# Storing the routing's comparisons and one-hots in groups of six token columns instead of eighteen

## The chip, the cores and the metric

The kernel runs on one core of a Trainium2 chip. The metric is the device time of one execution in microseconds (us); lower is better. TensorE (PE) does matmuls out of on-chip memory into PSUM, VectorE (DVE), ScalarE (ACT) and GpSimd (POOL) do elementwise work, SyncE (SP) issues most transfers.

## The reference

Three blocks follow each other: a masked attention (4 batches, 8 heads, 576 positions, 64 wide; local or strided mask of 32), a mixture of experts with greedy routing over its 2304 tokens, and a dense block on the result:

```python
logits = x @ w_gate                      # [2304, 8]
order = np.argsort(-logits.flatten())    # all (token, expert) pairs, best first
for idx in order:                        # greedy: expert e takes tok unless either is taken or full
    tok, e = (int(idx) // E, int(idx) % E)
    if assigned[tok] >= 0 or counts[e] >= cap:   # cap = 288
        continue
    assigned[tok] = e
    counts[e] += 1
for e in range(E):
    out[assigned == e] = np.maximum(x[assigned == e] @ w1[e], 0) @ w2[e]   # 512 -> 1024 -> 512
h = out @ w_in                           # 512 -> 2048
g = np.where(h > 0, h, np.exp(np.minimum(h, 0)) - 1)
return g @ w_out
```

## The kernel before

**Stages.** Attention fills the first 110 us or so. It leaves each token's eight logits on chip: 2304 tokens as 128 partitions by 18 columns. Then the routing runs in eight phases, each of which fills one expert, and the experts run one after the other in the order in which they are filled. Each expert's 288 tokens are gathered by an indirect DMA, go through the expert (matmuls of 288 columns) and then through the dense block (256, 384 or 512 columns). These matmuls are in single precision by a high and a low part, all issued from line 948. Phase 0 runs alone, with nothing else for PE to do; the routing of a later expert runs while an earlier expert is computed, its matmuls strewn into PE's stream.

**One routing phase.** A phase finds the logit at which the first expert is full by six digits, of 6, 6, 5, 5, 5 and 5 bits, that is K = 63 or 31 thresholds. For one digit DVE compares each token's digit with all thresholds at once (L711), which gives a 0/1 tile `cmp` (a part of `ohU`) in bf16. PE then counts per expert: one matmul for each token column c, whose weights are the column's one-hot of experts `oh[:, c, :]` and whose moving operand is the column's K comparisons (L740), 18 matmuls that add into one PSUM tile `pc`. DVE takes the digit from that (L742 to L757). When the threshold is known, the place of each token among the expert's 288 is worked out (L788 to L803), DVE makes the one-hot of places (L808, 96 wide) and PE uses it as weights, column by column, to bring the token numbers to their places (L818). After phase 3 half of the tokens are left, and `compact` moves them to 9 columns by two bursts of nine matmuls (L902) with the one-hot of L886 and L888 as weights. So phases 1 to 3 work on 18 columns, 4 to 7 on 9. Phase 7 has no digits, only the places.

**The layout.** The comparisons lie as [128, threshold, column], the 18 columns side by side for each threshold, also when only 9 are used. So DVE writes them in long runs, and PE reads the K comparisons of one column with a step of 18 numbers, 36 bytes:

```python
v.tensor_tensor(t['cmp'][:, :K, c0:c1], rb(t['cur'][:, c0:c1], K), self.kfull[:, :K, c0:c1], op=OP.is_ge)
nc.tensor.matmul(pc[:, :K], t['oh'][:, c, :], t['cmp'][:, :K, c], start=(c == 0), stop=(c == n - 1))
```

In phase 0 the columns go in two parts, 0 to 10 and 10 to 18, so that PE can begin on the first while DVE works on the second.

**The order of the work.** All queues are in order. While the program is built, a planner keeps an estimated clock: a cost for every operation (`D(...)` for DVE, 29 ns for a matmul of L740 and 27 ns for one of L818 behind phase 0), and each piece is emitted when the estimate says that its operands are there. DVE also turns the dense weights from float64 words into two parts (L217, L248, L253, shared with POOL), in gaps of the routing.

Of the kernel before, what the change touches and what calls it, by code (L numbers as in the profile page):

```python
# [28 lines left out]
KM = 63  # L29
RES, NSPILL, WORKERS, PREP_EARLY = 9, 4, 3, 7  # L30
# [9 lines left out]
# ---------------------------------------------------------------- host layout  # L40
def layout(inp):
    out = {}

    def rows(a):
        a = a.reshape(B, 2, 2, 2, S, D).transpose(0, 1, 3, 2, 4, 5)
        loc = a[:, 0]
        strided = a[:, 1].reshape(B, 2, 2, 18, 32, D).transpose(0, 1, 2, 4, 3, 5).reshape(B, 2, 2, S, D)
        return np.stack([loc, strided], 1).reshape(8, 2, 2 * S, D)

    qr, kr, vr = rows(inp['q']), rows(inp['k']), rows(inp['v'])  # L50
    out['qt'] = np.ascontiguousarray(qr.transpose(0, 1, 3, 2).reshape(8, 128, 4, 3, 96).transpose(0, 1, 3, 2, 4)).reshape(8, 128, 1152)
    kt = np.zeros((8, 2, D, 1184), np.float32)
    kt[..., 32:] = kr.transpose(0, 1, 3, 2)
    out['kt'] = kt.reshape(8, 128, 1184)
    vb = np.ones((8, 2, 32, 36, 65), np.float32)
    vb[..., :64] = vr.reshape(8, 2, 36, 32, D).transpose(0, 1, 3, 2, 4)
    out['vb'] = vb

    low = np.float32(-8e9)
    masks = np.zeros((128, 2, 9, 64), np.float32)  # L60
    qq, kk = np.arange(32)[:, None], np.arange(64)[None, :]
    for j in range(4):
        for i in range(9):
            b18 = (9 * j + i) % 18
            rk, rq = 32 * b18 - 32 + kk, 32 * b18 + qq
            near = (rk >= 0) & (rq >= rk) & (rq - rk < 32)
            same = (rk >= 0) & (rq >= rk) & (rq // 18 == rk // 18)
            masks[32 * j:32 * j + 32, 0, i] = np.where(near, 0, low)
            masks[32 * j:32 * j + 32, 1, i] = np.where(same, 0, low)
    out['mask'] = masks.astype(ml_dtypes.bfloat16)  # L70

    p, c = np.arange(128)[:, None], np.arange(18)[None]
    flat = 128 * (c // 2) + p
    n = 288 * (c % 2) + flat % 288
    t = 576 * (flat // 288) + 32 * (n % 18) + n // 18
    r = 576 * (flat // 288) + n
    out['tokp'] = np.stack([r // 128, r % 128, t // 128, t % 128], -1).astype(ml_dtypes.bfloat16)
    row = np.zeros((128, 16), np.float32)
    row[:, 0:3] = np.arange(3)
    row[:, 8:16] = 8 - np.arange(8)  # L80
    out['rowc'] = row.astype(ml_dtypes.bfloat16)
    out['ufull'] = np.broadcast_to(np.arange(96, dtype=np.float32)[None, :, None],
                                   (128, 96, 18)).astype(ml_dtypes.bfloat16)
    q = np.arange(128)
    out['tri'] = np.stack([q[:, None] <= q[None], np.ones((128, 128))], 1).astype(np.float32).astype(ml_dtypes.bfloat16)

    w1 = inp['moe_w1'].reshape(8, 4, 128, 8, 128).transpose(0, 3, 2, 1, 4).reshape(8, 8, 128, 512)
    w2 = inp['moe_w2'].reshape(8, 8, 128, 512)
    out['we'] = np.ascontiguousarray(np.concatenate([w1, w2], -1)).reshape(64, 128, 1024)
    wi = inp['moe2_w_in'].reshape(4, 128, 16, 128).transpose(2, 1, 0, 3).reshape(16, 128, 512)  # L90
    wo = inp['moe2_w_out'].reshape(16, 128, 512)
    out['wd'] = np.ascontiguousarray(np.concatenate([wi, wo], -1)).view(np.int64)
    out['wg'] = np.pad(inp['moe_w_gate'].reshape(4, 128, 8).transpose(1, 0, 2), ((0, 0), (0, 0), (0, 24)))
    return out


# ---------------------------------------------------------------- estimated clocks that order the work of the engines
class Line:
    """The tensor engine's program drives an estimated clock; jobs (generators that yield the time of their next piece)
    emit the other engines' work at the estimated time when its operands are there, so that no in-order queue blocks."""  # L100
# [66 lines left out]
    def idle(self, eng, cost):  # L167
        """Whether the engine is idle and no job that it is urgent for is about to want it."""
        u = min([j[1] for j in self.jobs if eng in j[3]], default=1e18)
        return self.free[eng] <= self.now + 80 and not (self.calm and eng != 'pool') and u > self.now + cost - SLACK  # L170
# [5 lines left out]
    def either(self, n):  # L176
        """GpSimd or the vector engine for n columns of a two-operand operation, whichever has room."""
# [8 lines left out]
class Bank:  # L186
    """One PSUM bank that several jobs share."""
# [14 lines left out]
# ---------------------------------------------------------------- dense weights: float64 words to two float32r parts  # L202
class Dense:
    """The 16 slices of the hidden dimension, [128, 512] of w_in and [128, 512] of w_out each, as high and low part:
    RES stay on chip in tiles of their own, as many as there are workers in the workers' tiles, the rest goes as float32
    words by DRAM."""
# [19 lines left out]
    def slice(self, f, k):  # L226
        """Float32 words from the float64 ones, then their high and low part."""
# [53 lines left out]
        t = 0  # L281
# [12 lines left out]
    def keep(self):  # L294
        """One more slice stays, in the tiles that the float32 words are worked out in."""
# [4 lines left out]
# ---------------------------------------------------------------- attention  # L300
# [282 lines left out]
# ---------------------------------------------------------------- greedy routing, one expert filled per phase  # L583
# [3 lines left out]
class Router:  # L587
    def __init__(self, nc, rp, I, identb, lg, line):
        self.nc, self.identb, self.lg, self.line, self.n = nc, identb, lg, line, 18

        def T(n, sh, d=F32):
# [3 lines left out]
        self.ufull = T("ufull", [128, 96, 18], BF)  # L595
        self.kfull = self.ufull[:, 1:KM + 1]
# [14 lines left out]
            ("vp", [128, 18, 12], BF), ("ohU", [128, 128, 18], BF), ("pif", [96, 12], F32), ("left", [128, 9, 8], F32))}  # L611
        self.t['cmp'] = self.t['ohU'][:, 0:KM]

    def start(self):
# [3 lines left out]
        self.nc.gpsimd.memset(self.t['ohU'][:, 96:], 0.0)  # L618
# [18 lines left out]
    def prelude(self, p, c0, c1):  # L637
        """Of the tokens in the columns c0 to c1: the best open expert, one-hot, and the digits of its logit."""
# [43 lines left out]
    def phase(self, p, res, bank, then=None):  # L682
        """Fills res['eidx'] ([1,1] int32, the expert that is filled) and res['idx'] ([96,3,2] int32, their
        rows of x and their tokens)."""
# [19 lines left out]
        if p < 7:  # L704
            parts = ((0, n),) if p else ((0, 10), (10, 18))
            for i in range(NS):
# [3 lines left out]
                for c0, c1 in parts:  # L710
                    v.tensor_tensor(t['cmp'][:, :K, c0:c1], rb(t['cur'][:, c0:c1], K), self.kfull[:, :K, c0:c1], op=OP.is_ge)  # L711
                    e.append(D(K * (c1 - c0), fast=2) + late)
# [24 lines left out]
                for (c0, c1), x in zip(parts, e):  # L737
                    yield x
                    for c in range(c0, c1):
                        nc.tensor.matmul(pc[:, :K], t['oh'][:, c, :], t['cmp'][:, :K, c], start=(c == 0), stop=(c == n - 1))  # L740
# [66 lines left out]
        for c0, c1 in parts if p < 7 else ((0, n),):  # L807
            v.tensor_tensor(t['ohU'][:, :96, c0:c1], rb(t['u'][:, c0:c1], 96), self.ufull[:, :, c0:c1], op=OP.is_equal)  # L808
            e.append(((c0, c1), D(96 * (c1 - c0), fast=2) + late))
# [5 lines left out]
        for (c0, c1), x in e:  # L815
            yield x
            for c in range(c0, c1):
                nc.tensor.matmul(pi[:, 0:12], t['ohU'][:, :, c], t['vp'][:, c, :], start=(c == 0), stop=(c == n - 1))  # L818
# [26 lines left out]
    def compact(self, bank):  # L845
        """Moves the tokens that are left, half as many as there were, to the first half of the columns, in their
        order: one-hot products over the three bfloat16 parts of their logits, which add up to them exactly."""
# [14 lines left out]
        for s in range(1, 18):  # L862
# [17 lines left out]
                        self.ufull[:, 0:9, 0][:, None, :].to_broadcast([128, 18, 9]), op=OP.is_equal)  # L880
# [5 lines left out]
        v.tensor_tensor(t['ohU'][:, :96], t['u'][:, None, :].to_broadcast([128, 96, 18]), self.ufull, op=OP.is_equal)  # L886
        yield D(96 * 18, fast=2)
        v.tensor_tensor(t['ohU'][:, 96:], t['cur'][:, None, :].to_broadcast([128, 32, 18]), self.ufull[:, 0:32], op=OP.is_equal)  # L888
# [3 lines left out]
        for h in range(2):  # L892
# [8 lines left out]
            for i in range(9):  # L901
                nc.tensor.matmul(px, t['ohU'][:, :, 9 * h + i], parts[:, i], start=(h == i == 0), stop=(h == 1 and i == 8))  # L902
# [16 lines left out]
# ---------------------------------------------------------------- experts and the dense block behind them  # L919
class Moe:  # L920
# [30 lines left out]
    # ---- weights of the experts and streamed dense slices, in the order of their use  # L951
# [54 lines left out]
    def warm(self, n):  # L1006
        """Keeps the tensor engine's clock up while it waits."""
# [4 lines left out]
    # ---- tokens of an expert  # L1012
# [37 lines left out]
    # ---- stage 1: relu(x w1) w2  # L1050
# [54 lines left out]
    # ---- stage 2: elu(y w_in) w_out  # L1105
# [175 lines left out]
def program(nc, tc, I, O):  # L1281
    with ExitStack() as ctx:
# [17 lines left out]
        M = Moe(nc, ctx, tc, I, x_d, O['out'], dr, identf, dense, line, bank, R.ufull.rearrange("p u c -> p (u c)"))  # L1300
# [55 lines left out]
```

## Time and profile before

| | |
|---|---|
| median of three runs | 880.23 us (877.32 to 880.27) |
| profiled execution, first to last instruction | 880.0 us |
| PE busy | 786.9 us (89%) |
| DVE busy | 551.3 us (63%) |
| matmuls of L740 | 594, of 63 columns (198) or 31 (396) |
| matmuls of L818 | 108 |

[...] A row of the timeline is: start, time from the first start to the last end, engine, line, operation, output and input with shapes, count (x18: eighteen in a row), and in brackets the engine's idle time before it and what ended it. A matmul's time there runs from its start to its result, so successive matmuls overlap; the cost of one in a burst is the distance of two starts, that is the time of the row less that of one matmul, divided by the count less one. A row of the stages is: stretch, its length, busy time (and count) of PE, PE's weight loads, DVE, ACT and POOL, granted clock, share of the DMA engines, GB/s. A row of the groups is: line, engine, operation, shapes, count, busy time, mean ns of one, idle time before.

### The profile page before, as it was taken

How to read it: one execution, taken by the hardware profiler on the slowest of the kernel's cores; microseconds unless marked ns; L12 is line 12 of the kernel's file. 1: busy time of each engine (PE TensorE's matmuls, PEld its weight loads, DVE VectorE, ACT ScalarE, POOL GpSimd, SP SyncE). 2: the span in 40 equal slices, each digit the busy share in tenths (PEclk: the TensorE clock that was granted, in tenths of full speed). 3: DMA queues.
4: the chain of work that ended last, by engine and by line, in shares of the span. 5: the costliest groups of instructions: out<-in, count | busy, mean ns of one | idle time of the engine just before them, and what ended most of it. 6: DMA issues, size and time to landing. Idle time of an engine off the chain costs nothing. (4 is left out here: it accounts for less than half of the span.)

```text
span 880.0 us, 16883 instructions
## 1 busy us (share of the span) xinstructions
PE 786.9 (89%) x6300; PEld 712.2 (81%) x6300; DVE 551.3 (63%) x1587; ACT 368.4 (42%) x770; POOL 324.8 (37%) x261
## 2 busy tenths in 40 slices
PE   3877844899899789969999999989999999999997
PEld 2656542888789779968999989989998999999896
DVE  4878876999987576678735763178438424533331
ACT  2766822555533332324334422434254345344221
POOL 5141313655535450263226320533174254325101
PEclk9898965888899989989999999989999999999999
DMA  9999627773513620432144122322342423212000
GB/s 211 295 257 284 182 71 163 263 260 114 117 61 120 111 85 14 64 120 74 60 76 145 60 40 25 120 85 96 28 168 96 52 100 110 80 60 85 1 1 36
DMA packets 50658, 96.58 MB, mean 110 GB/s; under 512 B 10256, under 2 KB 19984, under 8 KB 48016
## 3 DMA queue, kind: packets, MB, share of 16 engines
q1 hardware_dynamic: 47600, 86.07, 32.1%
q0 software_dynamic: 2976, 9.44, 7.2%
q8 instruction: 49, 0.80, 0.4%
q14 instruction: 33, 0.27, 0.1%
HBM read 83.94 MB, written 11.54 MB: 109 GB/s over the span
## 5 line engine op out<-in xcount | busy, mean ns | idle before, releaser
L217 POOL TENSOR_TENSOR wl<-raw,wh 128x512 fp32r<-128x512 f32 x161 | 212.4, 1335 | 281.1 <-ACT wh L989 279.6
L989 ACT ACTIVATE wh<-raw 128x512 fp32r<-128x512 f32 x178 | 111.0, 629 | 122.2 <-PE h L948 62.5
L1133 ACT ACTIVATE e<-h 128x256 f32<-128x256 f32 (+2 forms) x130 | 49.5, 390 | 132.6 <-PE h L948 130.2
L1139 ACT ACTIVATE ah<-e 128x256 fp32r<-128x256 f32 (+2 forms) x135 | 56.8, 423 | 111.6 <-DVE e L1137 109.3
L1135 DVE TENSOR_SCALAR e<-e 128x256 f32<-128x256 f32 (+2 forms) x138 | 54.8, 397 | 75.0 <-ACT e L1133 74.2
L1071 DVE SCALAR_TENSOR_TENSOR al<-h,ah 128x288 fp32r<-128x288 f32 x64 | 29.0, 454 | 96.0 <-ACT ah L1069 95.9
L948 PE MATMUL h<-yl,dense_hi 128*128 128x256 f32 (+1 forms) x284 | 86.3, 304 | 3.1 <-DVE yl L1099 3.1
L1141 DVE TENSOR_TENSOR al<-e,ah 128x256 fp32r<-128x256 f32 (+2 forms) x135 | 67.5, 506 | 31.2 <-ACT ah L1139 29.3
L948 PE MATMUL h<-yh,dense_lo 128*128 128x256 f32 (+1 forms) x284 | 86.5, 305 | 0.0
L948 PE MATMUL h<-yh,dense_hi 128*128 128x256 f32 (+1 forms) x284 | 86.3, 304 | 0.0
L948 PE MATMUL yo<-al,wh 128*128 128x288 f32 x256 | 77.4, 302 | 3.2 <-DVE al L1071 3.1
L948 PE MATMUL h<-xh,wh 128*128 128x288 f32 x256 | 76.9, 303 | 0.6 <-ACT xh L1042 0.6
L948 PE MATMUL h<-xh,wl 128*128 128x288 f32 x256 | 77.3, 304 | 0.0
L948 PE MATMUL yo<-ah,wh 128*128 128x288 f32 x256 | 76.8, 300 | 0.0
L948 PE MATMUL yo<-ah,wl 128*128 128x288 f32 x256 | 76.3, 298 | 0.2 <-POOL wl L217 0.2
L948 PE MATMUL h<-xl,wh 128*128 128x288 f32 x256 | 73.3, 301 | 0.0
L740 PE MATMUL pc<-r_ohU,r_oh 128*128 128x31 bf16 (+1 forms) x594 | 52.7, 255 | 16.5 <-DVE r_ohU L711 11.6
L217 POOL TENSOR_TENSOR g<-g,w 128x512 f32<-128x512 f32 x24 | 35.9, 1504 | 82.3 <-DVE g L253 39.3
L948 PE MATMUL yo<-dense_hi,al 128*128 128x512 f32 x156 | 63.8, 409 | 1.0 <-DVE al L1141 0.9
L948 PE MATMUL yo<-dense_lo,ah 128*128 128x512 f32 x156 | 62.5, 400 | 0.0
L740 PEld LDWEIGHTS <-r_oh 128*128 128x128 bf16 x594 | 44.6, 117 | 22.0 <-issue 17.7
L948 PE MATMUL yo<-dense_hi,ah 128*128 128x512 f32 x156 | 62.2, 398 | 0.0
(240 smaller groups left out, 2039.0 us busy)
## 6 DMA issues: line engine op xcount, KB each, us to landing
raw<-in_we SPq DMA_DIRECT2D x128, 256.0 KB, 2.7
w<-in_wd SPq DMA_DIRECT2D x16, 1024.0 KB, 6.6
raw<-dense_words SPq DMA_DIRECT2D x52, 256.0 KB, 3.0
kd<-in_kt SPq DMA_DIRECT2D x16, 296.0 KB, 8.1
vd<-in_vb SPq DMA_DIRECT2D x16, 292.5 KB, 10.8
qt<-in_qt SPq DMA_DIRECT2D x8, 576.0 KB, 7.8
x_d<-os SPq DMA_DIRECT2D x32, 144.0 KB, 6.3
dense_words<-g SPq DMA_DIRECT2D x4, 512.0 KB
```

What stands on the lines that cost most here:

```text
L217: (self.nc.vector if eng == 'dve' else self.nc.gpsimd).tensor_tensor(*a, **kw)
L740: nc.tensor.matmul(pc[:, :K], t['oh'][:, c, :], t['cmp'][:, :K, c], start=(c == 0), stop=(c == n - 1))
L948: self.nc.tensor.matmul(out, l, r, **kw)
L989: nc.scalar.activation(hi, r, AF.Copy)
L1071: nc.vector.scalar_tensor_tensor(al, ph, 0.0, ah.bitcast(F32), op0=OP.max, op1=OP.subtract)
L1133: nc.scalar.activation(e, x, AF.Exp)
L1135: nc.vector.tensor_scalar(e, e, 1.0, -1.0, op0=OP.min, op1=OP.add)
L1139: nc.scalar.activation(h, e, AF.Copy)
L1141: nc.vector.tensor_tensor(l, e, h.bitcast(F32), op=OP.subtract)
```

## The change

The tile `ohU` and the table `ufull` of the numbers 0 to 95 become [128, 3 groups, number, 6 columns]: in each group of six token columns, the six lie side by side for each number. PE now reads a column's comparisons, and its one-hot weights, with a step of 6 numbers, 12 bytes. DVE's comparison goes over whole groups with one more dimension, so that 9 columns are compared as 12, the last three with old data that no matmul reads. The parts of phase 0 become 0 to 12 and 12 to 18. The planner's costs of the comparisons follow their sizes; its costs of the matmuls stay. The rest of the diff takes away comments.

```diff
+GC = 6
-        self.ufull = T("ufull", [128, 96, 18], BF)
-        self.kfull = self.ufull[:, 1:KM + 1]
+        self.ufull = T("ufull", [128, 18 // GC, 96, GC], BF)
-            ("vp", [128, 18, 12], BF), ("ohU", [128, 128, 18], BF), ...
-        self.t['cmp'] = self.t['ohU'][:, 0:KM]
+            ("vp", [128, 18, 12], BF), ("ohU", [128, 18 // GC, 128, GC], BF), ...
+    def against(self, out, x, u0, u1, c0, c1, op, o0=None):
+        g0, g1 = c0 // GC, -(-c1 // GC)
+        n, o = u1 - u0, u0 if o0 is None else o0
+        self.nc.vector.tensor_tensor(out[:, g0:g1, o:o + n],
+                                     x[:, GC * g0:GC * g1].rearrange("p (g c) -> p g c", c=GC)[:, :, None, :]
+                                     .to_broadcast([128, g1 - g0, n, GC]), self.ufull[:, g0:g1, u0:u1], op=op)
+        return n * GC * (g1 - g0)
+    @staticmethod
+    def column(t, c):
+        return t[:, c // GC, :, c % GC]
-            parts = ((0, n),) if p else ((0, 10), (10, 18))
+            parts = ((0, n),) if p else ((0, 12), (12, 18))
-                    v.tensor_tensor(t['cmp'][:, :K, c0:c1], rb(t['cur'][:, c0:c1], K), self.kfull[:, :K, c0:c1], op=OP.is_ge)
-                    e.append(D(K * (c1 - c0), fast=2) + late)
+                    e.append(D(self.against(t['ohU'], self.t['cur'], 1, K + 1, c0, c1, OP.is_ge), fast=2) + late)
-                        nc.tensor.matmul(pc[:, :K], t['oh'][:, c, :], t['cmp'][:, :K, c], start=(c == 0), stop=(c == n - 1))
+                        nc.tensor.matmul(pc[:, :K], t['oh'][:, c, :], self.column(t['ohU'], c)[:, 1:K + 1], start=(c == 0), stop=(c == n - 1))
-            v.tensor_tensor(t['ohU'][:, :96, c0:c1], rb(t['u'][:, c0:c1], 96), self.ufull[:, :, c0:c1], op=OP.is_equal)
-            e.append(((c0, c1), D(96 * (c1 - c0), fast=2) + late))
+            e.append(((c0, c1), D(self.against(t['ohU'], self.t['u'], 0, 96, c0, c1, OP.is_equal), fast=2) + late))
-                nc.tensor.matmul(pi[:, 0:12], t['ohU'][:, :, c], t['vp'][:, c, :], start=(c == 0), stop=(c == n - 1))
+                nc.tensor.matmul(pi[:, 0:12], self.column(t['ohU'], c), t['vp'][:, c, :], start=(c == 0), stop=(c == n - 1))
```

The one-hots of `compact` (L886, L888) and its matmuls (L902) are changed in the same way.

## Rows read from the trace of the kernel before

**Rows 1.** The page: span, busy times, TensorE's granted clock by slices.
```profile
span 880.0 us, 16883 instructions
...
PE 786.9 (89%) x6300; PEld 712.2 (81%) x6300; DVE 551.3 (63%) x1587; ACT 368.4 (42%) x770; POOL 324.8 (37%) x261
...
PEclk9898965888899989989999999989999999999999
```
**Rows 2.** Stages: phase 0, then three stretches of the experts.
```profile
112.00:133.00 21.00, 9.31 (x108) 8.54 (x109) 17.28 (x90) 4.36 (x5) 2.56 (x2) 0.57 0.19 58
154.00:242.00 88.00, 78.55 (x553) 73.16 (x553) 85.37 (x194) 48.58 (x87) 51.87 (x36) 0.87 0.59 188
242.00:396.00 154.00, 136.96 (x1071) 127.42 (x1070) 110.52 (x334) 50.67 (x117) 61.02 (x49) 0.94 0.32 82
396.00:858.00 462.00, 455.57 (x3038) 424.68 (x3037) 238.16 (x732) 183.74 (x423) 162.06 (x132) 0.99 0.27 74
```
**Rows 3.** Groups by line and shape: the matmuls that the change touches.
```profile
L740 PE MATMUL pc<-r_ohU,r_oh 128*128 128x31 bf16 x396 | 27.7, 237 | 6.8 <-DVE r_ohU L711 6.4 <-DVE r_di L719 0.4
L740 PE MATMUL pc<-r_ohU,r_oh 128*128 128x63 bf16 x198 | 25.0, 292 | 9.7 <-DVE r_ohU L711 5.2 <-DVE xl L1044 2.8 <-DVE r_di L719 1.7
L818 PE MATMUL pi<-r_vp,r_ohU 128*128 128x12 bf16 x108 | 8.0, 206 | 5.2 <-DVE r_vp L810 2.8 <-POOL r_vp L810 2.4
```
**Rows 4.** Timeline of PE in phase 0.
```profile
114.80 2.23 PE L740 MATMUL pc<-r_ohU,r_oh 128*128 128x63 bf16 x18 [2.90 <-DVE r_ohU L711]
...
122.11 1.22 PE L740 MATMUL pc<-r_ohU,r_oh 128*128 128x31 bf16 x18 [1.34 <-DVE r_ohU L711]
...
133.92 0.68 PE L790 MATMUL pb<-r_ge,r_tri 128*128 128x36 bf16 x17
```
**Rows 5.** Timeline of PE among the experts.
```profile
159.20 0.29 PE L948 MATMUL h<-xh,wh 128*128 128x288 f32 x1
...
161.45 0.29 PE L948 MATMUL h<-xl,wh 128*128 128x288 f32 x1
...
213.80 0.58 PE L790 MATMUL pb<-r_ge,r_tri 128*128 128x36 bf16 x17
...
223.97 1.28 PE L818 MATMUL pi<-r_vp,r_ohU 128*128 128x12 bf16 x18 [1.62 <-DVE r_vp L810]
...
256.37 2.23 PE L740 MATMUL pc<-r_ohU,r_oh 128*128 128x63 bf16 x18
...
267.65 1.21 PE L740 MATMUL pc<-r_ohU,r_oh 128*128 128x31 bf16 x18
```
**Rows 6.** Timeline of DVE in phase 0, behind the bursts.
```profile
117.07 0.23 DVE L742 TENSOR_SCALAR_CACHE_REDUCE r_ok<-pc 128x63 bf16<-128x63 f32 x1 [1.14 <-PE pc L740]
...
123.36 0.19 DVE L742 TENSOR_SCALAR_CACHE_REDUCE r_ok<-pc 128x31 bf16<-128x31 f32 x1
...
129.52 0.19 DVE L742 TENSOR_SCALAR_CACHE_REDUCE r_ok<-pc 128x31 bf16<-128x31 f32 x1 [0.25 <-PE pc L740]
...
138.31 0.17 DVE L820 COPY r_pif<-pi 96x12 f32<-96x12 f32 x1 [0.29 <-PE pi L818]
```
**Rows 7.** Timeline of DVE: comparisons of different shapes.
```profile
114.27 0.48 DVE L711 TENSOR_TENSOR r_ohU<-r_cur,r_ufull 128x630 bf16<-128x630 bf16 x1
...
114.66 0.41 DVE L711 TENSOR_TENSOR r_ohU<-r_cur,r_ufull 128x504 bf16<-128x504 bf16 x1
...
255.34 0.74 DVE L711 TENSOR_TENSOR r_ohU<-r_cur,r_ufull 128x1134 bf16<-128x1134 bf16 x1
...
265.90 0.44 DVE L711 TENSOR_TENSOR r_ohU<-r_cur,r_ufull 128x558 bf16<-128x558 bf16 x1
...
400.62 0.58 DVE L711 TENSOR_TENSOR r_ohU<-r_cur,r_ufull 128x567 bf16<-128x567 bf16 x1
...
435.50 0.82 DVE L808 TENSOR_TENSOR r_ohU<-r_u,r_ufull 128x864 bf16<-128x864 bf16 x1
```
**Rows 8.** Timeline of DVE, POOL and PE in the second half of compact.
```profile
374.81 10.63 DVE L895 TENSOR_TENSOR r_oh<-r_dig,lg 128x648 bf16<-128x648 bf16 x1 [1.63 <-PE po L902]
...
374.81 9.93 POOL L217 TENSOR_TENSOR wl<-raw,wh 128x512 fp32r<-128x512 f32 x8
...
387.75 2.05 PE L902 MATMUL po<-r_oh,r_ohU 128*128 128x252 bf16 x9 [8.13 <-DVE r_oh L895]
```

More of the change, by code (lines that the diff above doesn't have):

```diff
@@ L81, in layout @@
     out['rowc'] = row.astype(ml_dtypes.bfloat16)
-    out['ufull'] = np.broadcast_to(np.arange(96, dtype=np.float32)[None, :, None],
-                                   (128, 96, 18)).astype(ml_dtypes.bfloat16)
+    out['ufull'] = np.broadcast_to(np.arange(96, dtype=np.float32)[None, None, :, None],
+                                   (128, 18 // GC, 96, GC)).astype(ml_dtypes.bfloat16)
     q = np.arange(128)
@@ L610, in __init__ @@
             ("t12", [128, 18], I32), ("u", [128, 18], BF), ("V", [128, 18, 3], BF),
-            ("vp", [128, 18, 12], BF), ("ohU", [128, 128, 18], BF), ("pif", [96, 12], F32), ("left", [128, 9, 8], F32))}
-        self.t['cmp'] = self.t['ohU'][:, 0:KM]
+            ("vp", [128, 18, 12], BF), ("ohU", [128, 18 // GC, 128, GC], BF), ("pif", [96, 12], F32), ("left", [128, 9, 8], F32))}
+    def against(self, out, x, u0, u1, c0, c1, op, o0=None):
[8 more added lines that the diff above has]
+        return t[:, c // GC, :, c % GC]
     def start(self):
@@ L617, in start @@
         self.nc.vector.memset(self.ge, 0.0)
-        self.nc.gpsimd.memset(self.t['ohU'][:, 96:], 0.0)
+        self.nc.gpsimd.memset(self.t['ohU'][:, :, 96:], 0.0)
     def load(self, I):
@@ L879, in compact @@
         v.tensor_tensor(V, t['t12'][:, :, None].to_broadcast([128, 18, 9]),
-                        self.ufull[:, 0:9, 0][:, None, :].to_broadcast([128, 18, 9]), op=OP.is_equal)
+                        self.ufull[:, 0, 0:9, 0][:, None, :].to_broadcast([128, 18, 9]), op=OP.is_equal)
         yield D(162)
@@ L885, in compact @@
         yield D(18)
-        v.tensor_tensor(t['ohU'][:, :96], t['u'][:, None, :].to_broadcast([128, 96, 18]), self.ufull, op=OP.is_equal)
+        self.against(t['ohU'], t['u'], 0, 96, 0, 18, OP.is_equal)
         yield D(96 * 18, fast=2)
-        v.tensor_tensor(t['ohU'][:, 96:], t['cur'][:, None, :].to_broadcast([128, 32, 18]), self.ufull[:, 0:32], op=OP.is_equal)
+        self.against(t['ohU'], t['cur'], 0, 32, 0, 18, OP.is_equal, 96)
         yield D(32 * 18, fast=2)
@@ L901, in compact @@
             for i in range(9):
-                nc.tensor.matmul(px, t['ohU'][:, :, 9 * h + i], parts[:, i], start=(h == i == 0), stop=(h == 1 and i == 8))
+                nc.tensor.matmul(px, self.column(t['ohU'], 9 * h + i), parts[:, i], start=(h == i == 0), stop=(h == 1 and i == 8))
             line.now += 9 * 106
@@ L1299, in program @@
         bank = Bank(mp, line)
-        M = Moe(nc, ctx, tc, I, x_d, O['out'], dr, identf, dense, line, bank, R.ufull.rearrange("p u c -> p (u c)"))
+        M = Moe(nc, ctx, tc, I, x_d, O['out'], dr, identf, dense, line, bank, R.ufull.rearrange("p g u c -> p (g u c)"))
         routed = [{} for _ in range(8)]
```

## The prediction

> **What bounds the kernel now.** I first read the page for the whole span: PE is the busiest engine, 89%, and from the experts on its granted clock is mostly at its upper level [rows 1]. A mean over stages with different limits says little, so next the stages [rows 2]. From 396 us to 858 us PE is busy 455.6 of 462 us: there the end is set by PE's in-order stream, and every ns that leaves it is a ns off the end. From 242 to 396 us it is 137.0 of 154 us, still mostly PE. From 154 to 242 us DVE is busy 85.4 of 88 us while PE has 9 us of gaps: two engines bound this stretch. In phase 0, 112 to 133 us, PE is busy 9.3 of 21 us and waits for each digit's DVE chain, which waits for each burst: a serial chain, whose length goes into the end.
>
> The third view is the groups: 594 matmuls of L740 and 108 of L818 [rows 3]. Their mean of 237 or 292 ns is a latency and no cost, so the fourth is PE's timeline, for distances of starts. A burst of 18 with 63 columns takes 2.23 us from first start to last end: (2.23 - 0.29)/17 = 114 ns each. With 31 columns it is (1.22 - 0.24)/17 = 57.6 ns [rows 4]. The difference is 56.5 ns for 32 columns, 1.77 ns a column, and 2.8 ns besides. So the moving operand sets the pace, not the 128x128 weight load before each matmul, which is the same for both. [...] Contiguous columns are another matter: 17 matmuls of 36 columns take 0.58 us among the experts, (0.58 - 0.18)/16 = 25 ns each, and 0.68 us in phase 0 [rows 4, 5]. What is slow is reading numbers that lie 36 bytes apart.
>
> **The change part by part.**
>
> *The moving operand's step, 36 to 12 bytes (L740).* The trace has no step of 12 bytes, so it is bounded. Above: no change, 1.77 ns a column. Below: contiguous, at the worst contiguous rate the trace has. That is 288 four-byte columns: from 159.20 to 161.45 us are 17 steps [rows 5], 132.4 ns each, less 2.8 is 0.45 ns a column. By it a matmul costs 31 ns (63 columns) or 25 (31 columns, the row of 36 being as low). Between the two I go by a reading of the same rows: 0.45 ns for 4 consecutive bytes is 1.80 ns for 16, nearly what one strided number costs (1.77). So I take it, as an estimate, that the operand comes in aligned blocks of 16 bytes, 1.77 ns each, whether one number of it is used or all. At 36 bytes each column is a new block; at 12 bytes four columns (48 bytes) touch three. That is 1.32 ns a column: 63 columns 114 -> 86 (-27.9), 31 columns 57.6 -> 43.9 (-13.7).
>
> [...]
>
> *The weights' step (L818).* Here the 128 weights are strided and the moving operand is 12 contiguous numbers: (1.28 - 0.21)/17 = 63 ns [rows 5], against at most 57.6 where weights are contiguous. The same quarter off the part above 3 ns: 63 -> 48 (-15); bounds 0 and -38 (25 ns). The 18 matmuls of L902 with 252 columns gain next to nothing and are left out.
>
> *PE's sum.* A phase of 1 to 3 has 36 matmuls of 63 columns, 72 of 31, 18 of L818: 1.00 + 0.99 + 0.27 = 2.26 us. Phases 4 to 6 have half, 1.13 us. Phase 7 has nine of L818, 0.14 us.
>
> *DVE's comparisons.* Rows of 18 that join to one run: 0.74 us for 1134 and 0.44 for 558, 0.52 ns a number and 0.15 us fixed; parts of 10 and 8 columns, with holes, 0.48 for 630 and 0.41 for 504 are on that line; rows of 9 are not, 0.82 for 864 and 0.58 for 567, 0.81 ns a number [rows 7]. Six is even like 8 and 10, so I take 0.52. Then phases 1 to 3 stay, and 4 to 6 compare 756 in 0.15 + 0.39 = 0.54 us for 0.58, and 1152 places in 0.75 for 0.82: nothing worth a term. The bound above, 0.81, adds 0.33 us to a 63-digit and 0.16 to a 31-digit. Its cover: a comparison ends before its burst's turn in PE's stream, as 265.90 + 0.44 = 266.34 before 267.65 us [rows 5, 7]; other bursts have less, down to the 0.3 us of the first burst of phase 2 (255.34 + 0.74 against 256.37). Without that cover it would cost some 1.3 us a phase.
>
> [...]
>
> *Phase 0.* The first part grows from 10 to 12 columns, so the burst begins later: 756 for 630 numbers is 0.07 us, 0.03 for a 31-digit. The two 63-bursts lose 18 x 27.9 = 0.50 us, DVE waited 1.14 us behind the first [rows 6], so all but the 0.07 arrives: 0.87 for two. Of the four 31-bursts (0.25 off each), two had DVE waiting 0.25 us, the row at 129.52 and its like; at 123.36 DVE came late from its dense work anyway [rows 6]. I count 0.2 twice and 0.05 twice. The places: 0.24 of the 0.29 us wait. Sum 1.6 us, all on the path to the first expert's gather.
>
> *Waits and queues.* No wait or queue is added, and no DMA is moved. In PE's stream a shorter burst brings forward the DVE chain behind it by as much as the expert's matmuls behind it, so the slack of the next burst stays. The planner's costs of the parts in phase 0 and of 12 columns in phases 4 to 7 shift by 0.05 to 0.15 us each, so pieces can be emitted in another order; I price that at 0 with the rival below.
>
> *How much arrives.* Phase 0: all, 1.6. Phase 1 lies where DVE is 97% busy: half, 1.1. Phases 2 and 3: PE's share there is 0.89, I take 0.85 of 4.52: 3.8. Phases 4 to 6: 0.95 of 3.39: 3.2. Phase 7: 0.1. Sum 9.8. Against the profiled execution's 880.0 us: 870.2; the median of the runs lies 0.2 above it: **870.4 us**, 1.1% less.
>
> **The rivals.**
>
> *A: a step of 12 bytes is as good as none (larger blocks).* Matmuls fall by 83, 32.6 and 38 ns: 6.0 us for each of phases 1 to 3, 3.0 for 4 to 6, 0.3 for 7. Phase 0 gains what DVE waits, 1.1 twice, 0.5 and 0.3. With the same shares 3.0 + 3.0 + 10.2 + 8.6 + 0.3 = 25: 855 us. For it: nothing in the trace fixes the block's size from above. Against: 16 bytes fits two unlike rows.
>
> *B: any step but one costs the same.* PE gains nothing, DVE next to nothing, phase 0 loses 2 x 0.07 + 4 x 0.03 = 0.3 us: 880.5. For it: the trace has one long step only. Against: the price of the strided column is that of 16 contiguous bytes, which a fixed penalty would hit by chance.
>
> *C, slower: trains of POOL in front of DVE.* In the second half of compact one product of DVE took 10.63 us because eight operations of POOL, released together when an output transfer had landed, ran 9.93 us from the same moment; PE lost 8.13 us [rows 8]. Shifted by some us, the trains that POOL lets go behind its transfers can meet other two-operand work of the routing. One more costs what PE lost here and nearly eats the gain (878.5); from the second on the kernel is slower: 870.4 + 16.3 = 886.7. For it: the emission order changes and a single one is seen now. Against: in 880 us only one hit the path, and the existing one can as well go.
>
> **How the numbers follow.** Forecast 0.58 (own range 866 to 876), A 0.14 (852 to 864), B 0.16 (877 to 881.5), C 0.12. A measurement here can tell about 0.5%, 4.4 us. Faster by more: nearly all of the forecast, 0.55, and A, with a little of the rest: 0.70. Slower by more: 0.12. The same: 0.18. For 8 in 10 the range drops C's slower end and the lower part of A: 857 to 881.5.
>
> **What would show it.** In PE's timeline a burst of 18 with 63 columns should take about 17 x 0.086 + 0.29 = 1.75 us, with 31 columns 0.99, of L818 1.02. At 0.8, 0.67 and 0.63 us it is A; at 2.23 and 1.2 it is B. Comparisons of 1134 at 0.74 us, of 756 at 0.54. DVE's wait before L742 in phase 0 falls from 1.14 to about 0.7 us. PE busy falls in phases 2 to 6 while its gaps stay. The prediction is wrong if the bursts shrink as said and the end doesn't follow: then PE's gaps from 154 to 396 us have grown, behind DVE (phase 1) or a train of POOL.

## The result, and the profile after

The changed kernel takes 886.81 us (median of 11 runs, 883.75 to 892.44) against 880.23 us (11 runs) for the kernel before, a ratio of 1.0091 with a 95% interval of 1.0063 to 1.0119: 0.9% slower, where 870.4 was forecast.

The page and the stages of the changed kernel, in the columns of [rows 1, 2]; the last stage is cut to expert 0's time, which turns out to matter:
```profile
span 888.3 us, 16888 instructions
...
PE 777.7 (88%) x6300; PEld 700.4 (79%) x6300; DVE 558.3 (63%) x1589; ACT 369.1 (42%) x770; POOL 321.9 (36%) x259
...
112.00:133.00 21.00, 8.64 (x127) 7.67 (x124) 16.11 (x95) 4.70 (x5) 0.00 (x0) 0.57 0.25 72
154.00:242.00 88.00, 70.16 (x514) 65.97 (x513) 78.28 (x185) 43.97 (x80) 47.10 (x32) 0.83 0.60 179
396.00:858.00 462.00, 451.42 (x3044) 419.87 (x3044) 246.89 (x741) 183.03 (x422) 164.44 (x134) 0.99 0.28 76
154.00:272.00 118.00, 94.14 (x654) 86.28 (x653) 104.28 (x238) 55.79 (x102) 60.76 (x41) 0.85 0.49 150
```
The same last stage in the kernel before:
```profile
154.00:272.00 118.00, 107.30 (x763) 99.69 (x763) 110.21 (x272) 60.20 (x113) 63.61 (x45) 0.91 0.50 161
```
PE does its work in 9.2 us less, and the end is later. From 154 to 242 us PE is busy 70.2 us where it was 78.6, at a granted clock (a share of full speed) of 0.83 where it was 0.87 [rows 2]: it stands still more and runs slower. In expert 0's stage it is busy 94.1 us where it was 107.3. From 112 to 133 us POOL does nothing at all, where it was busy 2.6 us, and DVE does 1.2 us less. (Phase 0 begins 1.7 us later in this run, at 116.54 against 114.80 us, so the stretches are not quite the same work.)

The groups, PE's timeline and DVE's in phase 0, and one comparison of phase 1:
```profile
L752 PE MATMUL pc<-r_ohU,r_oh 128*128 128x31 bf16 x396 | 22.4, 221 | 10.1 <-DVE r_ohU L618 10.0
L752 PE MATMUL pc<-r_ohU,r_oh 128*128 128x63 bf16 x198 | 19.4, 265 | 9.3 <-DVE r_ohU L618 6.5 <-DVE xl L1055 2.8
...
116.54 1.72 PE L752 MATMUL pc<-r_ohU,r_oh 128*128 128x63 bf16 x18 [2.96 <-DVE r_ohU L618]
122.93 0.98 PE L752 MATMUL pc<-r_ohU,r_oh 128*128 128x31 bf16 x18 [1.38 <-DVE r_ohU L618]
136.00 0.97 PE L829 MATMUL pi<-r_vp,r_ohU 128*128 128x12 bf16 x18 [2.54 <-POOL r_vp L821]
...
118.30 0.23 DVE L754 TENSOR_SCALAR_CACHE_REDUCE r_ok<-pc 128x63 bf16<-128x63 f32 x1 [0.70 <-PE pc L752]
123.94 0.19 DVE L754 TENSOR_SCALAR_CACHE_REDUCE r_ok<-pc 128x31 bf16<-128x31 f32 x1 [0.46 <-PE pc L752]
126.26 0.19 DVE L754 TENSOR_SCALAR_CACHE_REDUCE r_ok<-pc 128x31 bf16<-128x31 f32 x1 [0.44 <-PE pc L752]
...
164.79 0.73 DVE L618 TENSOR_TENSOR r_ohU<-r_cur,r_ufull 128x1134 bf16<-128x1134 bf16 x1
```
The bursts are as forecast: (1.72 - 0.27)/17 = 85 ns a matmul with 63 columns, (0.98 - 0.22)/17 = 45 with 31. DVE's wait behind the first is 0.70 us. But behind the third and fourth DVE now waits 0.46 and 0.44 us, where before it came late from dense work [rows 6]. That dense work is gone from these two gaps. In the layout of six with the old order (the first experiment below) it is there, two halves of L253:
```profile
121.07 0.68 DVE L253 SCALAR_TENSOR_TENSOR g<-w,g 128x512 uint32<-128x512 uint32 x1
124.23 0.69 DVE L253 SCALAR_TENSOR_TENSOR g<-w,g 128x512 uint32<-128x512 uint32 x1
```
So the order of the instructions is not the same, and "its costs of the matmuls stay", as the change is described above, is true only behind phase 0. The reason stands in a line that the diff does not touch. In phase 0 the routing tells the planner, by the number of columns in the last part, when its burst will be done:

```python
yield pe(n, 29) if p else line.now + (c1 - c0) * 40 + line.LAT      # behind L752; * 80 behind L829
```

Here c0 and c1 are the bounds of the last part, which went from 10 to 18 to 12 to 18. The estimate of a burst fell from 320 to 240 ns (places: 640 to 480); a burst of 31 takes 0.98 us. With a gap that looks 80 ns shorter the planner no longer puts 0.68 us of dense work into it.

### The profile page after: what moved, and what is told of

It is laid out like the page before. It is cut to its first block, busy times and chain, and to the rows that moved or that the text cites. A ratio compares the mean times of both kernels' runs of the same rounds, so it can differ in the third digit from the quotient of the medians.

```text
span 888.3 us, 16888 instructions
## 1 busy us (share of the span) xinstructions
PE 777.7 (88%) x6300; PEld 700.4 (79%) x6300; DVE 558.3 (63%) x1589; ACT 369.1 (42%) x770; POOL 321.9 (36%) x259
## 5 line engine op out<-in xcount | busy, mean ns | idle before, releaser
L1146 DVE TENSOR_SCALAR e<-e 128x256 f32<-128x256 f32 (+2 forms) x138 | 57.2, 414 | 79.8 <-ACT e L1144 79.4
L959 PE MATMUL h<-yl,dense_hi 128*128 128x256 f32 (+1 forms) x284 | 85.4, 301 | 2.2 <-DVE yl L1110 2.2
L959 PE MATMUL h<-yh,dense_hi 128*128 128x256 f32 (+1 forms) x284 | 84.9, 299 | 0.0
L959 PE MATMUL h<-yh,dense_lo 128*128 128x256 f32 (+1 forms) x284 | 84.8, 299 | 0.0
L959 PE MATMUL h<-xh,wl 128*128 128x288 f32 x256 | 77.9, 307 | 5.6 <-POOL wl L218 3.0
L959 PE MATMUL yo<-al,wh 128*128 128x288 f32 x256 | 77.5, 303 | 3.1 <-DVE al L1082 3.1
L959 PE MATMUL h<-xh,wh 128*128 128x288 f32 x256 | 77.3, 304 | 0.6 <-ACT xh L1053 0.6
L959 PE MATMUL yo<-ah,wh 128*128 128x288 f32 x256 | 77.0, 301 | 0.0
L959 PE MATMUL yo<-ah,wl 128*128 128x288 f32 x256 | 76.5, 299 | 0.5 <-POOL wl L218 0.5
L959 PE MATMUL h<-xl,wh 128*128 128x288 f32 x256 | 73.4, 302 | 0.0
L959 PE MATMUL yo<-dense_hi,al 128*128 128x512 f32 x156 | 64.2, 412 | 1.6 <-DVE al L1152 1.6
L959 PE MATMUL yo<-dense_lo,ah 128*128 128x512 f32 x156 | 62.4, 400 | 0.0
L959 PE MATMUL yo<-dense_hi,ah 128*128 128x512 f32 x156 | 62.3, 399 | 0.0
L1148 DVE TENSOR_TENSOR e<-e,h 128x256 f32<-128x256 f32 (+2 forms) x130 | 56.1, 431 | 5.3
L752 PE MATMUL pc<-r_ohU,r_oh 128*128 128x31 bf16 (+1 forms) x594 | 41.8, 235 | 19.4 <-DVE r_ohU L618 16.5
L959 PEld LDWEIGHTS h<-yl,dense_hi 128*128 128x128 f32 x284 | 54.7, 193 | 2.9 <-DVE yl L1110 2.9
```

The lines of the kernel that those rows point to most:

```text
L752: nc.tensor.matmul(pc[:, :K], t['oh'][:, c, :], self.column(t['ohU'], c)[:, 1:K + 1], start=(c == 0), stop=(c == n - 1))
L959: self.nc.tensor.matmul(out, l, r, **kw)
L1146: nc.vector.tensor_scalar(e, e, 1.0, -1.0, op0=OP.min, op1=OP.add)
L1148: nc.vector.tensor_tensor(e, e, x, op=OP.max)
```

## The experiments

**Layout and order apart.** Four kernels: the layout of six with all the planner's numbers as before; the old layout with the parts of 12 and 6 and the new numbers; and the layout of six with only one of the two numbers changed. The edits, against the changed kernel:

```diff
-                    e.append(D(self.against(t['ohU'], self.t['cur'], 1, K + 1, c0, c1, OP.is_ge), fast=2) + late)
+                    self.against(self.t['cur'], 1, K + 1, c0, c1, OP.is_ge)
+                    e.append(D(K * (c1 - c0 if p else 8 if c0 else 10), fast=2) + late)       # old comparison costs
-                yield pe(n, 29) if p else line.now + (c1 - c0) * 40 + line.LAT
+                yield pe(n, 29) if p else line.now + 8 * 40 + line.LAT                        # old estimate of a burst
```

> The groups of six, with the planner given the numbers of the kernel before (first part of phase 0 counted as 10 columns and the last as 8, 9 columns counted as 9), so that PE, ACT, POOL and SP get their instructions in exactly the order of the kernel before, and DVE too but for the comparisons' shapes. Theory O (the layout gains what was forecast, the new emission order costs more): 868 to 873 us, bursts of 18 at 85 ns (63 columns) and 44 ns (31). Theory L (something in the layout itself, such as DVE's extra dimension in the stretch where DVE is full, costs the time): 885 to 889 us, as the changed kernel.

> The layout of eighteen with the planner's numbers and the parts 0 to 12 and 12 to 18 of the changed kernel, so that all engines get their instructions in the order of the changed kernel. Theory O: slower than the changed kernel by what the layout gains, 893 to 898 us, bursts at 114 and 57 ns as before. Theory L: as the kernel before, 878 to 882 us.

> The groups of six; the planner gets the changed kernel's costs of the comparisons on DVE, but still counts the last part of phase 0 as 8 columns when it estimates the end of a burst (320 ns for the digits, 640 for the places). If that estimate of the burst's end is what moves the order: 868 to 873 us as the layout alone. If the comparisons' costs move it: 885 to 889 us.

> The groups of six; the planner gets the old costs of the comparisons, but counts the last part of phase 0 as 6 columns when it estimates the end of a burst (240 ns for the digits, 480 for the places), as the changed kernel does. If that estimate moves the order: 885 to 889 us, two of DVE's dense operations gone from phase 0 as in the changed kernel. If the comparisons' costs move it: 868 to 873 us.

The costs and the estimate of the one-hots of places are set in the same way. From phase 0 on, the trace of the first kernel has every engine's instructions in exactly the order of the kernel before, and the second has them in exactly the order of the changed kernel. The third leaves the order of the first, and the fourth that of the changed kernel, only in phase 4, some 300 us after the first burst.

| | median us | ratio to before (878.63 us, 23 runs) |
|---|---|---|
| layout only (old order) | 872.77, 12 runs | 0.9930 [0.9895, 0.9965] |
| order only (old layout) | 895.52, 6 runs | 1.0207 [1.0157, 1.0257] |
| layout, new comparison costs, old estimate | 868.88, 10 runs | 0.9903 [0.9866, 0.9940] |
| layout, old costs, new estimate | 887.16, 4 runs | 1.0105 [1.0048, 1.0163] |

The layout gains 5.9 us in the old order, and 895.52 - 887.16 = 8.4 us in the new one; the intervals overlap, so this shows no difference between the orders. The order costs 16.9 us in the old layout. It is the new estimate of the bursts that brings the loss: with it the layout takes 887.2, without it 872.8 or 868.9. The estimates for the digits and for the places were changed together, so which of the two counts is not shown.

**The reading in blocks of 16 bytes.** Groups of nine (18 bytes), three (6) and two (4), all in the layout's general form with the planner's old numbers:

```diff
-GC = 6
+GC = 9     # then 3, then 2
```

> Groups of nine columns (a step of 18 bytes), order of the kernel before, phase 0 in two parts of nine. Block theory (the operand comes in aligned blocks of 16 bytes at 1.77 ns): each column is a new block again, bursts at 114 ns (63 columns) and 57 ns (31), as with 36 bytes. Smooth theory (the price of a column grows with the step, 1.28 ns at 12 bytes, 1.77 at 36): about 1.4 ns a column, 91 and 46 ns.

> Groups of three columns (a step of 6 bytes), order of the kernel before. Block theory: eight columns touch three blocks, 0.66 ns a column, 45 ns for 63 columns and no less than the 25 ns of the fastest row for 31. Smooth theory: 1.1 ns, 72 and 37 ns. DVE compares in rows of three, odd like nine: 0.52 to 0.81 ns a number or more. The time: 858 to 868 us if the matmuls' gain arrives as with groups of six and DVE keeps its rate; not faster than the groups of six if DVE pays 1 ns a number.

> Groups of two columns (a step of 4 bytes), order of the kernel before. Block theory: four columns a block, 0.44 ns a column, 31 ns for 63 columns and 25 ns for 31. Smooth theory: above 0.9 ns a column, 60 ns. DVE in rows of two: 0.52 ns a number if rows of two still go two at a time, 1.05 if not. The time: 855 to 866 us in the first case, about 870 in the second.

One burst of each among the experts, in the order nine, three, three, two, two (timelines of PE):
```profile
250.09 2.27 PE L740 MATMUL pc<-r_ohU,r_oh 128*128 128x63 bf16 x18
```
```profile
255.30 0.97 PE L740 MATMUL pc<-r_ohU,r_oh 128*128 128x63 bf16 x18
264.22 0.63 PE L740 MATMUL pc<-r_ohU,r_oh 128*128 128x31 bf16 x18
```
```profile
249.71 0.71 PE L740 MATMUL pc<-r_ohU,r_oh 128*128 128x63 bf16 x18
265.70 0.60 PE L740 MATMUL pc<-r_ohU,r_oh 128*128 128x31 bf16 x18
```
With nine it is (2.27 - 0.30)/17 = 116 ns, as at 36 bytes: half the step, the same price. With three it is (0.97 - 0.22)/17 = 44, with two (0.71 - 0.19)/17 = 31. Blocks of 16 bytes at 1.77 ns and 2.8 ns besides give 114, 63 x 6/16 x 1.77 + 2.8 = 44.6, and 30.7. With 31 columns both end at 25 ns, the pace of the 36 contiguous columns of [rows 5].

In phase 0 these two short steps cost more. The first burst of each, three, then two:
```profile
115.92 1.14 PE L740 MATMUL pc<-r_ohU,r_oh 128*128 128x63 bf16 x18 [3.10 <-DVE r_ohU L612]
```
```profile
113.17 1.14 PE L740 MATMUL pc<-r_ohU,r_oh 128*128 128x63 bf16 x18 [2.96 <-DVE r_ohU L612]
```
That is (1.14 - 0.24)/17 = 53 ns for both, 0.84 ns a column, at a granted clock of 0.51 and 0.53 (112 to 133 us), where the bursts shown above ran at 1.00. By these runs the columns have a pace of their own that goes with the granted clock, and the blocks show only where they are slower than that: steps of 36, 18 and 12 bytes cost the same in phase 0 as among the experts, 2.23, 2.27 and 1.72 us a burst with 63 columns.

The kernels take 866.30 us (0.9862 [0.9833, 0.9892], three) and 860.77 us (0.9815 [0.9776, 0.9854], two), ratios to the kernel before in the same series; of nine there is one run, 872.74 us.

**True numbers for the planner.** If 320 ns are better than 240, are the measured ones better still?

```diff
-line.now + (c1 - c0) * 40 + line.LAT
+line.now + (1100 if i < 2 else 400) + line.LAT      # K is 63 for i < 2; 640 behind L829
```

> The groups of six with the changed kernel's costs of the comparisons, and the planner's estimate of what a burst of phase 0 still takes once its last part is there near the measured one: 1100 ns for 63 columns, 400 for 31, 640 for the places. Theory O says that dense work that fits in phase 0's gaps is taken off the stretch behind it: 862 to 870 us, faster than the order of the kernel before with this layout. If the order's effect is luck of a single emission, anything from 866 to 890.

878.42 us (12 runs), ratio 1.0014 [0.9986, 1.0042]: theory O missed, and only the wide range for an order whose effect is luck holds it. With more dense work let in, phase 0 takes 23.8 us from its first burst to L818, against 21.0 in the first experiment. A better estimate is not a better order.

**What the order costs.** The time is lost while expert 0 is computed. The starts of PE's main products (L948, L959 after), each counted from its own run's first burst of phase 0, in us:

| main product | layout, old order | layout, new order (changed kernel) | difference |
|---|---|---|---|
| first | 37.4 | 36.7 | -0.8 |
| 76th | 51.9 | 59.0 | +7.1 |
| 391st | 125.3 | 130.6 | +5.3 |
| 451st | 135.5 | 149.5 | +14.0 |
| last | 753.1 | 765.2 | +12.0 |

There are two steps that last, at the start of expert 0 and near its end. (One profiled run of each: two runs with the same order this far, those of the layout with old and with new comparison costs, are 2.1 us apart at the first main product, so a difference of some 2 us says nothing.) PE's waits from 154 to 272 us (us in total, times, longest), first in the new order, then in the old:
```profile
PE px L1049 <- DMA rows<-x_d,r_iall: 7.5, 1, 7.5
PE pc L752 <- DVE r_ohU L618: 5.0, 4, 2.1
PE h L959 <- ACT parts L280: 3.1, 1, 3.1
PE h L959 <- DVE wl L218: 2.6, 1, 2.6
PE h L959 <- POOL wl L218: 2.4, 1, 2.4
```
```profile
PE px L1038 <- DMA rows<-x_d,r_iall: 4.6, 1, 4.6
PE pc L740 <- DVE r_ohU L612: 3.6, 3, 2.2
PE yo L948 <- DVE al L1141: 2.5, 1, 2.5
```
New are waits for the low part of expert 0's weights (wl) and for the parts of the last dense slices. And more is lost than the waits, for the granted clock around them is lower: 0.56 to 0.76 from 155 to 170 us, where it is 0.95 to 1.00 in the old order. PE in pieces of 5 us (stretch, length, busy and count, granted clock, DMA), new order, then old:
```profile
155.00:160.00 5.00, 4.46 (x20) 0.58 0.37 121
160.00:165.00 5.00, 1.74 (x8) 0.76 0.26 93
165.00:170.00 5.00, 4.42 (x32) 0.56 1.00 381
255.00:260.00 5.00, 1.43 (x5) 0.82 0.19 63
260.00:265.00 5.00, 3.67 (x14) 0.50 0.15 52
```
```profile
155.00:160.00 5.00, 5.00 (x38) 0.95 0.98 377
160.00:165.00 5.00, 4.01 (x37) 1.00 0.63 244
165.00:170.00 5.00, 4.08 (x31) 1.00 0.10 39
255.00:260.00 5.00, 5.00 (x35) 1.00 0.14 45
260.00:265.00 5.00, 5.00 (x56) 1.00 0.31 117
```
After the wait at 257 us PE runs at a granted clock of 0.50, in the old order at 1.00. From the 431st main product to the 441st it takes 6.8 us in the new order and 1.4 in the old one; 3.9 of these 5.4 us are the two waits for the parts.

Which work is late? The first theory (D) was DVE's dense work, pushed out of phase 0. Two kernels, new and old order, leave out DVE's dense steps of the last eight slices, those begun after phase 0 starts:

```diff
+        self.begun = getattr(self, 'begun', -1) + 1; full = self.begun < 8
-        nc.vector.tensor_scalar(gi, gi, 3, None, op0=OP.logical_shift_left)
+        if full: nc.vector.tensor_scalar(gi, gi, 3, None, op0=OP.logical_shift_left)
...
-            nc.vector.scalar_tensor_tensor(gn, even[:, 512 * n:512 * n + 512], 29, gn,
+            if full: nc.vector.scalar_tensor_tensor(gn, even[:, 512 * n:512 * n + 512], 29, gn,
```

> The changed kernel (layout of six, its own order), except that of the last eight dense slices, those begun after phase 0 starts, the vector engine's three operations that shift and or the words together (0.68 us each, 24 in all) are left out; the planner still counts them, so every other instruction stands where it stood. Those eight slices hold other words, which costs no engine anything. It is paired with the next run, the same of the old order. Theory D (the new order costs because dense preparation is pushed out of phase 0 into the first expert's stage, where the vector engine then makes main products and the routing's bursts wait): with the late preparation relieved, the difference between the two orders, 14.4 us in the full kernels, falls to within 3 us, and this kernel comes to about 865 to 870 us. Rival G (the order itself costs, by where bursts, gather and transposes stand in TensorE's queue): the difference stays at 12 to 15 us, and this kernel takes 878 us or more.

> The layout of six in the old order, with the same 24 operations of the last eight dense slices left out (the same words of eight slices are then other words). Theory D: 863 to 869 us, within 3 us of its pair in the new order. Rival G: 12 to 15 us below its pair. Both: the last main product comes at most 10 us before that of the full kernel of this order (872.8 us), since 16 us of vector engine work are gone and TensorE is busy 88% of the span.

881.04 us (10 runs, 1.0019 [0.9982, 1.0056]) and 867.67 us (4 runs, 0.9851 [0.9788, 0.9913]): 13.4 us apart. D falls as it was put, and rival G's numbers hold. But the relief was too narrow to clear dense preparation as a whole: the slices that slipped were in work when phase 0 began (two halves like those of L253 still stand in phase 0 of the first of the two), and ScalarE's and GpSimd's part of the rest stayed. So the next pair leaves out all preparation, on every engine, of the last 11 slices; a third pair leaves it in and takes the waits for low parts away.

```diff
+        self.begun = getattr(self, 'begun', -1) + 1; full = self.begun < 5
-        nc.scalar.activation(g, odd, AF.Abs, scale=2.0 ** -112)
+        if full: nc.scalar.activation(g, odd, AF.Abs, scale=2.0 ** -112)
...
+        if not full: hi = lo = self.first
```
```diff
-        return w
+        return w if key[1] else (w[0], w[0], w[2])      # expert 0: the high part in place of the low
```

> The layout of six in the changed kernel's order, with all the preparation of the last 11 dense slices (those begun from phase 0 on) left out on ScalarE, the vector engine and GpSimd; only their loads stay, and the first slice's high part stands in for theirs in the products. The planner still counts the work, so what is left stands in the same order. Paired with the same of the old order. Theory D2 (the dense preparation that the new order pushes out of phase 0 comes late on three engines' in-order queues: first expert 0's weights wait behind it, then the last products wait for the parts): both losses go, and the difference between the orders, 14.4 us in the full kernels, falls to within 3 us. Theory D3 (only the second loss, the wait for the parts, is dense preparation; the first is where the burst stands in TensorE's queue): 5 to 9 us are left. Rival G (places in the queues alone): 12 to 15 us are left.

> The same left out of the layout of six in the old order (872.8 us in full). All theories: 860 to 868 us, since the vector engine, which is busy nearly throughout expert 0's stage, gets free there. Against its pair in the new order: within 3 us by D2, 5 to 9 us less by D3, 12 to 15 us less by G.

> The changed kernel's order in full, but expert 0's products take the high part of a weight where the low part belongs; the low parts are still worked out, nobody waits for them. So the two waits of TensorE for them in expert 0 (2.45 and 2.60 us in the changed kernel) are gone. If they, and the half clock behind the first of them, are the first loss: 5 to 8 us off the changed kernel's 887, that is 879 to 882 us. If TensorE then only waits for the burst behind them: 885 us or more.

> The same in the old order, whose trace has no wait for a low part in expert 0: 872 to 873 us, as with the low parts, by all theories. The difference to its pair in the new order, 14.4 us in the full kernels, is 6 to 9 us if the first loss is the low parts' and 12 to 15 us if not.

| | new order | old order | apart by |
|---|---|---|---|
| no late dense preparation | 864.14, 4 runs, 0.9826 [0.9760, 0.9892] | 860.15, 4 runs, 0.9803 [0.9736, 0.9870] | 4.0 |
| no wait for low parts | 887.84, 4 runs, 1.0126 [1.0049, 1.0203] | 873.06, 10 runs, 0.9928 [0.9891, 0.9964] | 14.8 |

The low parts were not it. Without them PE stands at the same place for something else, the first comparison of phase 1. The longest waits of that kernel (new order):
```profile
PE px L1038 <- DMA rows<-x_d,r_iall: 7.7, 1, 7.7
PE pc L740 <- DVE r_ohU L612: 6.1, 1, 6.1
```
Without late dense preparation 4.0 us are left, between the ranges of D2 (within 3) and D3 (5 to 9), and the second step is gone: there, new minus old is 9.1 us at the 391st main product and 8.7 at the 451st. The first step is still there, 0.4 us at the 31st and 6.0 at the 76th. PE's timeline at the first burst of phase 1, new order, then old:
```profile
158.49 1.72 PE L743 MATMUL pc<-r_ohU,r_oh 128*128 128x63 bf16 x18 [2.35 <-DVE r_ohU L615]
```
```profile
156.23 1.73 PE L743 MATMUL pc<-r_ohU,r_oh 128*128 128x63 bf16 x18
```
Counted from the first burst of phase 0 both start after 46 us. But in the new order 33 main products stand before it in PE's queue, in the old one 52; before the rows of the next expert (px) it is 319 and 361. PE runs out of work that stands ahead of a step for which it must wait, and then runs slower: from 160 to 165 us its granted clock is 0.66, in the old order 1.00. The same happens again at the rows of expert 1, in the new order, then in the old:
```profile
PE px L1041 <- DMA rows<-x_d,r_iall: 7.5, 1, 7.5
```
```profile
PE px L1041 <- DMA rows<-x_d,r_iall: 4.0, 1, 4.0
```
New minus old is 4.9 us at the 319th main product, 13.1 at the 320th, behind the new order's wait, and 9.1 at the 391st, when the old order has waited too. In the full kernels it is 4.5, 12.6 and 5.3.

So the two steps have different causes. The second is late dense preparation: it goes when that is left out. The first, by these traces, is the place of phase 1's bursts and of the gather in PE's queue; no run moved these alone, and the orders of the other engines and of the loads differ too, so this is argued and not shown. How the 14 us divide is not settled: the two profiled runs without late preparation are 7.8 us apart counted from the first burst (that of the old order, 854.62 us, is 5.5 below its median), the medians 4.0, with intervals of some 6 us each.

**The best version.** Groups of two, old estimate of a burst, the planner told the true sizes of the parts of phase 0, 12 and 6 columns. The 9 columns of phases 4 to 6, which groups of two compare as ten, are still counted as nine:

```diff
-                    e.append(D(K * (c1 - c0 if p else 8 if c0 else 10), fast=2) + late)
+                    e.append(D(K * (c1 - c0), fast=2) + late)
```

> Groups of two token columns, with the old estimate of a burst (320 and 640 ns for every part of phase 0) and the planner told the comparisons' true sizes, as the run with the new costs had it at groups of six. If the costs' part of the change is worth what it seemed at six (872.8 against 868.9, 3.9 us, intervals that overlap), this is at 855 to 859 us; if that was nothing, 860.8 again, as the groups of two with the old costs; if a new order of phases 1 to 7 does harm, above 864.

862.53 us (4 runs, 0.9802 [0.9740, 0.9864]), beside 860.77 with the old costs. The traces of the two have the same instructions in the same order from phase 0 on, so this is a second measurement of one program and not a test of the costs. At six, the costs moved the order only from phase 4 on, where 9 columns were counted as 12, and this run doesn't do that. Whether the 3.9 us there are real stays open. Groups of two with the planner's numbers untouched are the best here, about 2% faster than the kernel before in both series.

## Why the prediction was wrong

**The step that failed** is "pieces can be emitted in another order; I price that at 0 with the rival below". It looked for the shift in the costs of the comparisons, which turned out to do no harm (868.88 us without the new estimate). It missed that the parts of phase 0 also enter the estimate of a burst's end, and it had no price for another order but one train of POOL. Measured, the order costs 16.9 us in the old layout and 14.4 in the new (887.16 against 872.77 us), more than the whole gain forecast.

**The moving operand's step** was right. 85 ns for 86 and 45 for 43.9, and the further steps (18, 6, 4 bytes) fall where blocks of 16 bytes put them. Rivals A and B are out by the same rows. But the way to the block's size had luck in it. The prediction took 0.45 ns a four-byte column as a price of reading and found that four of them make one strided number. It is a pace that goes with TensorE's granted clock: the same products, a few us earlier in the kernel before, at a granted clock of 0.50 (155 to 159 us):
```profile
155.14 0.44 PE L948 MATMUL h<-xh,wl 128*128 128x288 f32 x1
155.38 0.44 PE L948 MATMUL h<-xh,wh 128*128 128x288 f32 x1
```
They come 240 ns apart there, 0.83 ns a column, against 132 ns at 1.00 (159.20 to 161.45 us), while a burst with 63 columns at 36 bytes takes 2.23 us at both clocks: at 0.50 in phase 0 (114.80 to 117.03 us) and at 1.00 among the experts (256.37 to 258.60 us) [rows 4, 5]. That four times 0.45 is near 1.77 is chance; what fixes the 16 bytes is the runs at 18, 12 and 6. (At 4 bytes the blocks' 30.7 ns and 63 columns at 0.45 ns with the 2.8, 31 ns, can't be told apart.)

**The weights' step** was right too, (1.00 - 0.19)/17 = 48 ns among the experts in phases 1 to 3 (217.01 and 302.26 us).

**DVE's comparisons** were right: 1134 numbers in 0.73 us for a forecast of 0.74; 756 alone 0.54.

**Phase 0** was right in the old order: from the first burst to the start of L818 it takes 21.0 us after 22.2, some 1.2 us less, where the terms up to there come to 1.4 (the 0.24 of the places lies behind that start). In the changed kernel it is 19.5, but that is dense work put off.

**How much arrives** was too high for this order of things: 9.8 us forecast, 5.9 measured in the old order (interval some 3 us either way). There the layout is 5.2 us ahead at the 361st main product and 0.3 at the 381st. In between PE waits for the rows of expert 1, which come only 2.6 us earlier: 4.6 us instead of 1.9. Behind the longer wait its granted clock is 0.76 from 235 to 240 us, where it was 1.00. So the sum alone would have been some 4 us off, inside the range of 866 to 876.

**Rival C** named a slower end by emission order, but through POOL's trains in compact. There is still one of these in the changed kernel, with 8.1 us of PE idle, as in [rows 8]. The mechanism was another.

**What would show it** did show it: "the bursts shrink as said and the end doesn't follow: then PE's gaps from 154 to 396 us have grown".

## What to carry to other kernels

Where a planner orders the work, every size that feeds an estimate is part of a change, also in lines that the diff leaves alone: follow the changed size to each estimate first, and set the instruction order before against the one after before trusting a sum of savings. To price a change, hold the order fixed and change the layout, then the reverse. For an operand that TensorE reads with a step, count the 16-byte blocks it touches, 1.77 ns each by these runs, and set their price against the pace of the columns at the clock that is granted there, here 0.46 ns a contiguous column at 1.00 and 0.83 at 0.50.

## What the runs showed of the hardware

- TensorE's moving operand in bf16: a matmul with 63 columns cost 114 ns at a step of 36 bytes, 116 at 18, 85 at 12, 44 at 6 and 31 at 4. A price of 1.77 ns for each 16-byte block, with 2.8 ns besides, fits these; with 31 columns, 6 and 4 bytes both ended at 25 ns. The bursts at the first three steps took the same in phase 0 and among the experts (2.23, 2.27 and 1.72 us with 63 columns); at 6 and 4 bytes a matmul cost 53 ns in phase 0, at a granted clock of 0.51 and 0.53. Strided weights: 63 ns at 36 bytes, 48 at 12.
- DVE's comparison lost nothing in rows of two: 1728 numbers took 1.05 us in runs of 18, of six and of two (means of 3 or 4), but 1.35 us in rows of three.
- Two waits of PE, of 3.1 and 2.35 us, were followed by some us at a lower granted clock: 0.50 from 260 to 265 us behind 3.1 us, 0.66 from 160 to 165 us behind 2.35 us in the kernel without late preparation. The three waits of PE around 257 us (1.3, 3.1 and 0.8 us, 5.2 together) went with a step of 8.7 us between the 391st and the 451st main product.
- The first burst of phase 0, behind the attention, starts anywhere from 109.7 to 116.5 us in the profiled runs, and these two ends are kernels with the same order (order only, and the changed kernel). A single span can't tell 5 us here; medians of several runs can, and times counted from the first burst help, to some 2 us.
